# A new written order for a five-engine attention and feed-forward kernel, with five more summed sets

## The chip, the cores and the metric

The kernel runs on one core of a Trainium2 chip. Five engines work side by side from queues of their own: TensorE (PE in the profile; its weight loads PEld), VectorE (DVE), ScalarE (ACT), GpSimd (POOL), and SyncE (SP), which here issues nearly all DMAs. The metric is the device time of one execution in microseconds (us). Before the change three runs took 684.30, 684.40 and 684.44 us; the median is 684.4.

## The reference

Two branches work on the same x of 2048 rows and 640 columns and are mixed row by row:

```
g = sigmoid((x * gate_w).sum(-1))
a = softmax_attention(x @ wqkv, 32 heads of 20 columns) @ wo
h = x @ w1 + b1                       # 1536 columns
b = (h * tanh(softplus(h))) @ w2      # Mish
out = g * a + (1 - g) * b
```

The scores are 32 matrices of 2048 x 2048. Everything is bf16 on the way in and out.

## The kernel before

**Tiling.** Four heads make a quartet; there are 8 quartets and 4 query chunks of 512 columns, so 32 groups G of one quartet and one chunk. Within a group there are 16 key blocks j of 128 rows, and for each the four heads t. A *score tile* is one (G, j, t): a matmul with 32 weight rows and 128 weight columns that writes 128 x 512 values into one of seven PSUM banks (`score`, L1073). The heads of a quartet sit in four row groups of 32 of TensorE's array.

**Two ways to an exponential.** Most key blocks go to ScalarE: one activation (L1091, step `x`) reads one, two or three neighbouring banks and writes E in SBUF. Five or so blocks of every group, "sets", go to VectorE instead: `d_unit` (step `D`) makes the score tile and a tensor_scalar (L586) writes a scaled score as int16, whose bits read as bf16 are a power of two with a piecewise linear fraction. To come closer to the exponential, the kernel uses shifted copies of the int16 tile, made on GpSimd by adding a constant to four values at a time (L616, `add_shift`). A plain set uses the tile and two shifted copies as three right-hand sides, the copies with values of V scaled by fixed ratios (`VD`). A *summed* set adds the tile and its first copy on VectorE (L640, `total` in `d_sum`) and shifts the original once more, so it has two right-hand sides. The flag is the last number of a `d` step. A summed set has other constants (`SHIFT2`, `BETA2`).

**Products with V.** Step `V` (`emit_pv`, L1108) is four matmuls with 21 weight columns each, one per head, in four column groups of the array; they add into bank 7. The 21st column of V is one, so the row sum of the softmax comes with it. When the last product of a group is in, `normalise` puts four VectorE instructions and a store on record: a transpose (L1137), a reciprocal (L1144), a product (L1151) and the stores to `o_dram`.

**The rest of the matmuls** are in 184 chains: projections to q, k, v (`dense_chain`, `v_chain`, `first_k_chain`), w1 (`h_chain`), w2 (`b_chain`) and wo (`wo_chain`). Each chain fills one bank with 1 to 20 products (`product`, L663: four matmuls of 32 weight columns) and is then emptied by VectorE (L850 with the bias for w1, L752 for q and k, L808 for v, L895 for w2, L972 for wo). Mish runs twice on ScalarE over 12288 columns (L871, step `m`).

**The order** is written out by hand. A string, ORDER, is read step by step, and every step issues its instructions to the engines' queues in that order:

- `S2,4`: two score tiles for ScalarE into banks 4 and 5; `x2`: one activation over the two oldest of these
- `D24,14,3,6`: the score tile of group 24, block 14, head 3 into bank 6 for VectorE; `d24,13,0`: take a set
- `C5,6`: begin chain 5 in bank 6; `F`: its next product
- `V14,1`: the products of block 14 with right-hand side 1 (-1 is E)
- `y142`: the 142nd VectorE instruction that was put on record; `p31,6`: the 31st shift on GpSimd, into buffer 6 (-1 is in place)
- `l`, `q`, `k`, `o`, `b`, `e`: loads on SP's queue, `m`: Mish, `H`: products with zero weights

Each queue runs strictly in its order; an instruction waits until what it reads is written and what it overwrites has been read. So the string fixes what stands behind what on each of the engines.

The steps that matter below: `b1f`, the bias as f32, was made by a cast (L849) inside the emptying of the first w1 chain, directly ahead of L850. Its source `b1bf` is loaded by step `l2` (`load_late`, L487) together with the first tile of w1. In the string, group 23's reciprocal is `y767`, its L1151 `y771`; group 24's L1151 is `y803`.

Of the kernel before, what the change touches and what calls it, by code (L numbers as in the profile page):

```python
# [9 lines left out]
P = 128  # L10
ACT = mybir.ActivationFunctionType
ALU = mybir.AluOpType
F32 = mybir.dt.float32
# [6 lines left out]
S2,4 S2,2 C0,6 S2,0 x2 x2 F F F F F C1,5 F y1 y3 C2,4 F x2 y4 C3,5 S2,2 F x2 y5 C4,4 S2,0 F x2 y2 y6 C6,5 S2,2  # L20
x2 F F F F F F F d2,3,0 F F F F F F F F F F F F F C5,6 F F S2,0 S2,3 F F F x2 y7 d0,6,0 y8 y9 x2 y10 y11 y12
C7,2 F F F F F S2,0 x2 S2,5 C8,3 V0,-1 F F F F F F F F F F F F F F F F F F F F y13 y14 y15 x2 V1,-1 S3,0 C9,4
F F F F F S2,5 x3 x2 y16 d0,8,0 y17 y18 y19 d1,5,0 V2,-1 C10,6 V4,-1 S3,0 S2,3 V3,-1 V5,-1 F F F F F x3 x2 y20
C11,5 F S3,0 F F F F F d1,0,0 F F F F F F F D0,15,3,3 x3 D0,15,0,4 F F F F F F F C12,6 F F S3,0 F F F y21 y23
y24 y25 y26 y27 y22 x3 D0,15,2,5 S2,3 x2 y29 d3,4,0 y28 V6,-1 V7,-1 S3,0 C13,5 F F D0,14,3,6 S2,3 F F F x2 q1
y30 y31 x1 x2 C14,0 F F F V9,-1 D0,15,1,6 S2,1 F F F F F F F F F F F S2,3 D0,14,0,5 F V8,-1 y32 x2 q2 y33 x2
D0,14,1,6 S2,1 F F F F F y34 x2 y35 V10,-1 C15,6 S3,3 y36 y37 y38 y39 F F F F F D0,14,2,2 S2,0 F F F F F v0,0
V11,-1 V15,0 y44 y43 y40 p1,1 x3 x2 D1,15,1,5 S3,2 y41 y42 x3 V14,0 V15,1 y45 D1,15,0,6 y46 S2,0 V12,-1 C16,5
F F F F F F S3,2 D1,15,2,6 F F F F p2,7 p3,1 p4,6 d1,2,0 l0 y47 V14,1 V15,2 x2 x3 S2,0 D1,14,0,6 y48 y49 y50
C17,5 V14,2 V13,-1 D1,15,3,2 S2,3 d2,6,0 x2 y51 l1 F F F d1,1,0 x2 y52 D1,14,1,6 S2,0 F F x2 p5,7 S2,2  # L30
D1,14,2,4 x2 p6,8 y53 y54 y55 y56 l2 V0,-1 V1,-1 S2,0 D1,13,0,6 C18,5 F F S3,2 x2 y58 y57 F F F S2,0 D1,13,1,6
# [277 lines left out]
def kernel(  # L309
# [1087 lines left out]
```

## Time and profile before

| what | value |
| --- | --- |
| median of 3 runs | 684.4 us (684.30 to 684.44) |
| profiled execution, first to last instruction (span) | 681.8 us |
| median beyond the span | 2.6 us |
| PE busy | 672.8 us (99%) |
| ACT busy | 666.7 us (98%) |
| DVE busy | 597.3 us (88%) |
| POOL busy | 354.0 us (52%) |
| granted TensorE clock | 0.999 |

The page gives the span of the profiled execution and no other time of it; the 2.6 us are what the timed runs take beyond that span. In the timeline a row has the start, the length, the engine, the line, the operation, what it writes and reads, how often it stands in the row, and in brackets the idle time before it with what ended it. Neighbouring instructions of one line are merged into one row. Matmuls are pipelined: the next one starts well before the first has ended, so the distance of starts says more than lengths.

### The profile page before, as it was taken

How to read it: one execution, taken by the hardware profiler on the slowest of the kernel's cores; microseconds unless marked ns; L12 is line 12 of the kernel's file. 1: busy time of each engine (PE TensorE's matmuls, PEld its weight loads, DVE VectorE, ACT ScalarE, POOL GpSimd, SP SyncE). 2: the span in 40 equal slices, each digit the busy share in tenths (PEclk: the TensorE clock that was granted, in tenths of full speed). 3: DMA queues.
4: the chain of work that ended last, by engine and by line, in shares of the span. 5: the costliest groups of instructions: out<-in, count | busy, mean ns of one | idle time of the engine just before them, and what ended most of it. 6: DMA issues, size and time to landing. Idle time of an engine off the chain costs nothing.

```text
span 681.8 us, 24517 instructions
## 1 busy us (share of the span) xinstructions
PE 672.8 (99%) x10355; PEld 234.2 (34%) x10355; DVE 597.3 (88%) x1033; ACT 666.7 (98%) x692; POOL 354.0 (52%) x349
## 2 busy tenths in 40 slices
PE   8999999999999999999999999999999999999997
PEld 4433333323323443333333222222243333333334
DVE  5689989898999889899888988999999988799896
ACT  6999999999999999999999999999999999999996
POOL 5135446454454535565645654456646654466453
PEclk9999999999999999999999999999999999999999
DMA  8444322213312211111231223221232122131221
GB/s 171 118 89 126 81 43 53 53 38 63 89 26 52 49 44 36 26 35 34 43 97 33 43 53 74 64 55 33 56 92 60 21 48 29 41 66 35 60 87 60
DMA packets 128542, 40.47 MB, mean 59 GB/s; under 512 B 94960, under 2 KB 127872, under 8 KB 128432
## 3 DMA queue, kind: packets, MB, share of 16 engines
q1 hardware_dynamic: 126032, 38.29, 25.5%
q8 instruction: 81, 1.33, 0.9%
q10 hardware_dynamic: 2400, 0.62, 0.4%
q14 instruction: 29, 0.24, 0.1%
HBM read 22.29 MB, written 12.78 MB: 51 GB/s over the span
## 4 chain that ended last, share of the span: by engine, by line
PE 89%; ACT 7%; DVE 2%; issue 1%; POOL 0%; DVEq 0%; ACTq 0%
PE Sp L1108 30%; PE Sp L1073 30%; PE Sp L663 29%; ACT E L1091 5%; ACT big L871 2%; DVE T L586 0%; PE Sp L515 0%; PE Sp L1336 0%; DVE T L1151 0%; DVE ot L1353 0%; PE Sp L1217 0%; PE Sp L1123 0%; ACT L1091 0%; PE Sp L1199 0%; ACT big L966 0%
## 5 line engine op out<-in xcount | busy, mean ns | idle before, releaser
L1091 ACT ACTIVATE E<-Sp 128x1024 bf16<-128x1024 f32 (+2 forms) x674 | 634.7, 1127 | 4.4 <-PE Sp L1073 3.7
L616 POOL INT64_ADD T<-T x334 | 344.1, 1042 | 314.2 <-DVE T L586 208.5
L586 DVE TENSOR_SCALAR T<-Sp 128x512 int16<-128x512 f32 x668 | 440.2, 682 | 56.1 <-PE Sp L1073 45.7
L1073 PE MATMUL Sp<-qT,kT 32*128 32x512 bf16 x2048 | 259.5, 384 | 2.9 <-ACT E L1091 1.0
L1073 PEld LDWEIGHTS <-kT 32*128 32x128 bf16 x2048 | 70.1, 91 | 244.9 <-issue 240.4
L1108 PE MATMUL Sp<-E,VA 128*21 128x512 bf16 x1380 | 128.0, 382 | 0.0
L1108 PE MATMUL Sp<-T,VD 128*21 128x512 bf16 x1288 | 117.9, 382 | 0.1
L663 PE MATMUL Sp<-w_sb,big 128*32 128x320 bf16 x1536 | 72.9, 302 | 0.2 <-DVE T L586 0.2
L663 PE MATMUL Sp<-xT,w1t 128*32 128x512 bf16 x960 | 72.2, 382 | 0.0
L1108 PEld LDWEIGHTS <-VA 128*21 128x21 bf16 x2048 | 43.9, 90 | 57.3 <-issue 48.4
L1108 PE MATMUL Sp<-T,VA 128*21 128x512 bf16 x668 | 63.5, 382 | 0.0
L663 PE MATMUL Sp<-xT,ws 128*32 128x512 bf16 x720 | 52.2, 382 | 0.0
L1108 PEld LDWEIGHTS <-VD 128*21 128x21 bf16 x1288 | 29.8, 90 | 38.6 <-issue 32.6
L663 PEld LDWEIGHTS <-big 128*32 128x32 bf16 x1536 | 32.9, 95 | 29.0 <-issue 21.8
L850 DVE TENSOR_SCALAR big<-Sp,b1f 128x512 bf16<-128x512 f32 x48 | 35.6, 741 | 1.8 <-PE Sp L663 1.2
L663 PE MATMUL Sp<-wv,xT 128*32 128x81 bf16 (+2 forms) x960 | 31.0, 257 | 0.0
L663 PEld LDWEIGHTS <-w1t 128*32 128x32 bf16 x960 | 19.8, 95 | 25.4 <-issue 17.4
L752 DVE CAST st<-Sp 128x512 bf16<-128x512 f32 x36 | 24.5, 681 | 2.6 <-PE Sp L663 2.4
L663 PE MATMUL Sp<-wo_sb,od 128*32 128x320 bf16 (+1 forms) x608 | 26.3, 301 | 0.1
L1137 DVE STREAM_TRANSPOSE T<-Sp 128x512 f32<-128x512 f32 x32 | 22.7, 709 | 2.6 <-PE Sp L1108 2.4
L663 PEld LDWEIGHTS <-xT 128*32 128x32 bf16 x960 | 18.8, 96 | 10.8 <-issue 7.7
L663 PEld LDWEIGHTS <-ws 128*32 128x32 bf16 x720 | 15.3, 95 | 19.4 <-issue 12.1
(76 smaller groups left out, 196.8 us busy)
## 6 DMA issues: line engine op xcount, KB each, us to landing
w1t<-in_B_w_dram SPq DMA_DIRECT2D x24, 320.0 KB
q_dram<-st SPq DMA_DIRECT2D x20, 128.0 KB
b_dram<-bt SPq DMA_DIRECT2D x16, 160.0 KB
bl<-b_dram SPq DMA_DIRECT2D x16, 160.0 KB
qT<-q_dram SPq DMA_DIRECT2D x124, 20.0 KB
o_dram<-T SPq DMA_DIRECT2D x120, 20.0 KB
out_dram<-ot SPq DMA_DIRECT2D x15, 160.0 KB
kT<-k_dram SPq DMA_DIRECT2D x28, 80.0 KB
```

The lines of the kernel that those rows point to most:

```text
L586: nc.vector.tensor_scalar(out=dst.bitcast(I16), in0=src, scalar1=inv_sqrt_dh * LOG2E * 128.0, scalar2=127.0 * 128.0 + (BETA2 if two else B ...
L616: nc.gpsimd.int64_add(dst[:, :].bitcast(I64), src[:, :].bitcast(I64), n * 0x0001000100010001)
L663: nc.tensor.matmul(out_[k : k + 32], lhsT=lhsT[:, k : k + 32], rhs=rhs, tile_position=(0, k), **kw)
L752: nc.vector.tensor_copy(out=res["st"][:, :], in_=ps[:, :])
L850: nc.vector.tensor_scalar(out=big[:, pair_of(c, ft), (ft % 2) * QC : (ft % 2 + 1) * QC], in0=ps[:, :], scalar1=b1f[:, ft : ft + 1], scalar ...
L871: nc.scalar.activation(v, v, ACT.Mish)
L1073: nc.tensor.matmul(ps_cols, lhsT=kT[p][32 * t_ : 32 * t_ + 32, j * P : (j + 1) * P], rhs=qT[G][32 * t_ : 32 * t_ + 32, :], tile_position=( ...
L1091: nc.scalar.activation(E[:, x : x + n, :], allb[:, k0 : k0 + n, :], ACT.Exp, scale=inv_sqrt_dh,)
L1108: nc.tensor.matmul(acc[32 * t_ : 32 * t_ + DH + 1, :], lhsT=lhsT, rhs=rhs, start=(pv_done[G] == 0), stop=(pv_done[G] == pv_total[G] - 1), ...
L1137: nc.vector.transpose(out=st["T1"][:, :, :].rearrange("p b r -> p (b r)"), in_=acc[:, :])
```

## The change

The ORDER string is replaced as a whole: 5819 steps become 6236. Both have the same 1380 score tiles for ScalarE and 668 for VectorE, the same 184 chains with 1220 products, the same loads. What differs:

- the places of nearly all steps; 740 of the ScalarE score tiles are now steps of their own (`S1,3`), none were before
- 688 activations instead of 674: 55 over one bank, 574 over two, 59 over three (before 31, 580, 63)
- 17 summed sets instead of 12: (10,11) and (21,12) become plain, (1,15), (12,12), (13,11), (15,10), (22,11), (26,12) and (26,13) are summed
- 44 shifts on GpSimd in place instead of 13
- the bias cast is a VectorE instruction of its own, put on record by step `l2`, which stands earlier
- a chain knows its bank, so products of several chains can alternate (`F134 F144`), where before a chain ended before the next began
- the code can also run a product row group by row group (`run_part`, step `f`); the new ORDER has no such step

```diff
-S2,4 S2,2 C0,6 S2,0 x2 x2 F F F F F C1,5 F y1 y3 C2,4 F x2 y4 C3,5 S2,2 F x2 y5 C4,4 S2,0 F x2 y2 y6 C6,5 S2,2
-x2 F F F F F F F d2,3,0 F F F F F F F F F F F F F C5,6 F F S2,0 S2,3 F F F x2 y7 d0,6,0 y8 y9 x2 y10 y11 y12
...
-D3,10,1,2 D4,14,0,1 S2,5 q6 p32,1 x2 V11,0 F F S2,3 V11,1 V8,-1 y140 y141 p33,7 x2 y142 D4,15,1,6 D4,13,0,5
-S2,1 V11,2 V10,0 p34,2 y143 x2 S2,3 D4,15,2,0 y144 x2 y145 V10,1 V9,-1 S2,1 D4,14,1,6 C32,5 F V10,2 y146 x2
...
-F F F F x2 b6 y765 x2 D24,14,2,5 D24,14,1,4 S2,2 p249,3 x2 y767 y770 d24,0,0 y771 y766 d25,6,0 y769 y768 V15,0
-V0,-1 S2,0 D24,14,3,6 D24,14,0,4 y773 x2 S2,2 C135,5 F F F F S2,0 D24,13,2,4 x2 x2 d24,3,0 y772 y774 F F F F
...
-D25,13,1,5 S2,2 F V10,-1 S2,0 D25,13,2,4 F F F F y797 x2 y798 x2 y799 S2,2 D25,12,0,5 F F F S2,0 D25,13,3,4
-p259,0 p260,2 p261,5 p262,1 x2 y800 y801 y802 x2 F V15,0 V15,2 S2,2 D25,12,1,5 V1,-1 d25,8,0 V14,0 y804 x2
-S2,0 D25,12,2,6 D25,12,3,4 y803 y805 p263,2 x2 d25,6,0 V14,2 V15,1 D25,11,0,5 S2,2 y806 y807 x2 V2,-1 V0,-1
...
+S1,0 S1,2 x1 S1,3 S1,6 C0,1 x2 C1,0 S1,5 C2,2 C6,4 F0 F0 F0 F0 F0 y1 F F y2 x1 F1 F2 x1 S1,3 C4,5 S1,1 x1 S1,6
+F x1 F6 y3 C3,3 y4 y5 F y6 C8,3 x1 S3,0 x3 S1,5 F6 F6 C5,6 F6 F6 F F F6 F d0,8,0 x1 F6 F8 F6 F6 F6 F F8 F8 F6
...
+S3,0 D3,10,3,5 x2 x1 y134 V3,-1 V13,2 V4,-1 D3,12,2,6 C34,0 S2,3 V13,1 y20 F F y135 D4,15,0,5 x2 S1,1 x2 y122
...
+S1,5 D4,14,0,2 S1,6 F F y144 F S1,3 p31,6 p32,5 x2 S1,4 V11,0 p33,7 y145 y146 V8,-1 D4,13,0,5 x2 S2,1
+D4,15,1,6 x2 V11,1 V11,2 y148 y147 S1,3 D4,15,2,0 S1,4 p34,2 V10,0 V10,1 D4,14,1,6 y149 C32,5 x2 d4,6,1 S1,1
...
+y768 y767 p249,6 S1,5 x2 S2,2 S2,0 C132,6 F V10,2 F F F F F x2 F F F F F x2 y770 F S1,2 D24,14,1,4 S1,3 y769
+V0,-1 H D24,14,2,5 S1,0 y772 y773 S1,1 V15,0 d24,7,0 D24,14,0,4 x2 D24,14,3,6 y774 x2 S2,2 C135,5 F y775 F x2
+y776 F y771 F F D24,13,2,4 S2,0 F F d25,6,0 F S1,2 D24,13,0,6 S1,3 F y777 F p251,3 x2 p252,4 y778 F p250,-1
...
+D25,13,1,5 F y800 F p261,5 y801 F F D25,13,2,4 x2 S1,0 x2 S1,1 V10,-1 V11,2 F y802 y803 y804 S2,2 D25,12,0,5
+p262,1 F x2 F S1,0 d25,8,0 q28 D25,13,3,4 x2 S1,1 F y806 y807 F V15,0 F S1,2 D25,12,1,5 S1,3 V14,2 x2 V1,-1
+p260,-1 S1,0 y808 x2 D25,12,3,6 S1,1 D25,12,2,4 V15,2 V14,1 S2,2 y809 x2 p263,2 x2 D25,11,0,5 y810 d26,5,0
...
 class Chain:
 
 
-    def __init__(self, start, due, pieces, evac):
+    def __init__(self, start, due, n, fn, evac, last=None, cols=512):
         self.start, self.due = start, due
-        self.pieces = deque(pieces)
-        self.evac = evac
+        self.fn, self.evac, self.last = fn, evac, last
+        self.n, self.first, self.rows, self.told = n, True, {}, None
+        self.whole, self.top = 0, n
+        self.ps, self.cols = None, cols
+
+    def done(self):
+        return self.whole == self.top and all(len(r) == 4 for r in self.rows.values())
...
             if i == 2:
                 nc.sync.dma_start(b1bf, B_b1.rearrange("(ft p) -> p ft", p=P))
+                dve(lambda: nc.vector.tensor_copy(b1f, b1bf))
             load_w1(i - 2)
         else:
             ft = slice(2 * (i - 4), 2 * (i - 4) + 2)
...
+    def product(ch, out_, lhsT, rhs, row, start=None):
+        if start is None:
+            start, ch.first = ch.first, False
+        if row is not None:
+            r = slice(32 * row, 32 * row + 32)
+            mm = nc.tensor.matmul(
+                out_, lhsT=lhsT[r, :], rhs=rhs[r], tile_position=(32 * row, 0),
+                start=start, stop=ch.done(), skip_group_check=True,
+            )
+            if ch.told is not None:
+                tc.add_manual_dep(mm.ins, ch.told.ins.name, told, reason="parts of one bank")
+            if not ch.done():
+                ch.told = nc.sync.nop()
+                tc.add_manual_dep(ch.told.ins, mm.ins.name, told, reason="parts of one bank")
+            return
         for k in range(0, P, 32):
             nc.tensor.matmul(
-                out_[k : k + 32], lhsT=lhsT[:, k : k + 32], rhs=rhs, tile_position=(0, k), **kw
+                out_[k : k + 32], lhsT=lhsT[:, k : k + 32], rhs=rhs, tile_position=(0, k),
+                start=start, stop=ch.done(), skip_group_check=True,
             )
...
             def copy():
-                if (ft, c) == (0, 0):
-                    nc.vector.tensor_copy(b1f, b1bf)
                 nc.vector.tensor_scalar(
                     out=big[:, pair_of(c, ft), (ft % 2) * QC : (ft % 2 + 1) * QC], in0=ps[:, :],
                     scalar1=b1f[:, ft : ft + 1], scalar2=None, op0=ALU.add,
...
-    def run_piece():
-        ch = chain[0]
-        ch.pieces.popleft()()
-        if not ch.pieces:
-            ops, done = ch.evac()
+    def run(ch, k, row):
+        if ch.ps is None:
+            ch.ps = bank_ap(ch.bank, [P, ch.cols])
+        ch.fn(ch, k, row)
+        if ch.done():
+            if ch.last:
+                ch.last()
+            ops, done = ch.evac(ch)
             for f in ops[:-1]:
                 dve(f)
             dve(ops[-1], done)
+
+    def run_piece(i=None):
+        ch = chain[0] if i is None else chains[i]
+        ch.whole += 1
+        run(ch, ch.whole - 1, None)
+
+    def run_part(i, row):
+        ch = chains[i]
+        for k in sorted(ch.rows, reverse=True):
+            if row not in ch.rows[k]:
+                break
+        else:
+            ch.top -= 1
+            k = ch.top
+            ch.rows[k] = set()
+        ch.rows[k].add(row)
+        run(ch, k, row)
...
     def begin(k, bank):
-        chain[0], chain_bank[0] = chains[k], bank
+        chain[0] = chains[k]
+        chains[k].bank = bank
 
     steps = {
         "q": load_q,
         "V": emit_pv,
         "C": begin,
         "F": run_piece,
+        "f": run_part,
         "H": heat,
         "y": vector,
         "Y": vector,
```

More of the change, by code (lines that the diff above doesn't have):

```diff
@@ L668, in transpose_chain, with piece @@
         c, u = divmod(s, NU)
-        def piece():
-            ps = box["ps"] = bank_tile([P, KT * P], BF16)
+        def piece(ch, k, row):
+            ps = ch.ps = bank_ap(ch.bank, [P, KT * P], BF16)
             for kt in range(KT):
@@ L686, in evac @@
             return [copy], None
-        return Chain(start, due, [piece], evac)
+        return Chain(start, due, 1, piece, evac)
     strip_left = {}
@@ L760, in evac @@
             return [copy], done
-        return Chain(start, due, mm_pieces(KT, piece), evac)
+        return Chain(start, due, KT, piece, evac, last)
     def rows_in(kind, p):
@@ L861, in evac @@
             return [copy], done
-        return Chain(start, due, mm_pieces(KT, piece), evac)
+        return Chain(start, due, KT, piece, evac, last)
     act_q = deque()
```

669 lines of the change are left out of this document (335 added, 334 removed).

## The prediction

> **What bounds the kernel now.** I read the page first: busy shares, then the chain that ended last.
>
> ```profile
> span 681.8 us, 24517 instructions
> PE 672.8 (99%) x10355; PEld 234.2 (34%) x10355; DVE 597.3 (88%) x1033; ACT 666.7 (98%) x692; POOL 354.0 (52%) x349
> PE 89%; ACT 7%; DVE 2%; issue 1%; POOL 0%; DVEq 0%; ACTq 0%
> PE Sp L1108 30%; PE Sp L1073 30%; PE Sp L663 29%; ACT E L1091 5%; ACT big L871 2%; DVE T L586 0%; PE Sp L515 0%; PE Sp L1336 0%; DVE T L1151 0%; DVE ot L1353 0%; PE Sp L1217 0%; PE Sp L1123 0%; ACT L1091 0%; PE Sp L1199 0%; ACT big L966 0%
> ```
>
> Three matmul lines share 89% of the chain equally: TensorE's own queue sets the end, with ScalarE nearly as full and VectorE at 88%. A busy PE of 99% hides small waits, because the ends of matmuls are modelled. So I priced the queue by turns, from starts in the timeline. Four column-tiled matmuls (L1108, L663) run side by side as one product turn; up to four row-tiled score matmuls (L1073) as one score turn.
>
> ```profile
> 20.74 0.60 PE L1073 MATMUL Sp<-qT,kT 32*128 32x512 bf16 x5
> 21.27 0.61 PE L1108 MATMUL Sp<-E,VA 128*21 128x512 bf16 x8
> ...
> 300.26 0.61 PE L1108 MATMUL Sp<-T,VD 128*21 128x512 bf16 x8
> 300.70 0.39 PE L663 MATMUL Sp<-xT,ws 128*32 128x512 bf16 x4
> 301.02 0.39 PE L1073 MATMUL Sp<-qT,kT 32*128 32x512 bf16 x3
> 301.34 0.62 PE L663 MATMUL Sp<-xT,ws 128*32 128x512 bf16 x8
> ```
>
> Eight L1108 matmuls, two turns, take 300.70 - 300.26 = 0.44, so 0.22 a turn. The single turn at 300.70 takes 0.32, because a score turn follows: a change of kind costs 0.10. A score turn followed by a product turn also takes 0.32 (301.02 to 301.34). Five score matmuls, which need two turns, take 21.27 - 20.74 = 0.53: a second score turn in a row costs 0.21.
>
> Counted along the written order before: 649 score turns, 1280 product turns of 512 columns, 616 of 320, 160 narrower ones, four transposes, and 1277 changes of kind. A turn of 320 columns costs (232.89 - 232.21) / 5 = 0.136:
>
> ```profile
> 8.47 0.60 PE L1073 MATMUL Sp<-qT,kT 32*128 32x512 bf16 x6 [0.44 <-DVE qT L1236]
> ...
> 231.34 1.05 PE L663 MATMUL Sp<-xT,ws 128*32 128x512 bf16 x16
> 232.21 0.85 PE L663 MATMUL Sp<-wv,xT 128*32 128x320 bf16 x20
> 232.89 1.25 PE L663 MATMUL Sp<-xT,ws 128*32 128x512 bf16 x20
> ...
> 674.62 1.53 PE L1336 MATMUL Sp<-wo,O 128*128 128x320 bf16 x8
> ```
>
> 1929 x 0.22 + 616 x 0.136 + 1277 x 0.10 = 636; the 160 narrow turns, bounded by 0.136 each, add at most 22. So 636 to 658 of the 666 us between the first score turn (8.47) and the closing products (674.62) is TensorE's own work, and **8 to 30 us is waiting**. That is all an order can win; the start and the tail, 8.5 + 7.2 us, keep their code.
>
> **The change, part by part.** Times are against the profiled span of 681.8; the timed runs have a median of 684.4, 2.6 longer, which I carry over unchanged.
>
> Turns. Five more sets are summed: each loses one product turn on L1108 (three right-hand sides become two), 5 x 0.22 = 1.10 gained. Counted along the new order there are 652 score turns, three more at 0.21, 0.63 lost, and again exactly 1277 changes of kind, though 740 of the 1380 tiles for ScalarE are now issued singly (before none): most stay neighbours on TensorE's queue. Sum **-0.47**.
>
> The bias cast (L849) leaves the path. Before, it stood directly ahead of the first L850:
>
> ```profile
> 96.99 0.81 DVE L849 CAST b1f<-b1bf 128x12 f32<-128x12 bf16 x1
> 97.91 0.75 DVE L850 TENSOR_SCALAR big<-Sp,b1f 128x512 bf16<-128x512 f32 x1
> ...
> 98.18 0.90 PE L1073 MATMUL Sp<-qT,kT 32*128 32x512 bf16 x3
> 99.01 0.40 PE L1108 MATMUL Sp<-T,VD 128*21 128x512 bf16 x4
> ```
>
> L850 empties bank 0, and the third score of the turn at 98.18 writes bank 0: the turn lasts 0.90 instead of 0.39, 0.51 of waiting. In the new order the cast stands some 6 us of work earlier, between the emptying of a q/k product and the int16 cast (L586) of a score tile in bank 5. That bank is written again six turns and two changes, some 2.1, after it was filled; 0.75 (an emptying like L850's) + 0.81 + 0.62 (L586, from 2.47 for four, below) is 2.2, so some of it comes back: 0 to 0.4, all 0.81 if nothing covers it. I take 0.2. Its DMA and the first w1 tile's move well ahead on SP's queue, before the loads of q, k and further strips; the q tile they delay is not read until the second group. **-0.51 + 0.20**.
>
> Normalising behind the score casts. Twice VectorE does part of a normalisation ahead of score casts, and TensorE waits:
>
> ```profile
> 516.68 0.25 DVE L1144 RECIPROCAL rec<-T 128x16 f32<-128x16 f32 x1
> 516.85 1.16 DVE L640 TENSOR_TENSOR T<-T 128x2048 bf16<-128x2048 bf16 x1
> 517.93 0.48 DVE L1151 TENSOR_TENSOR T<-T,rec 128x320 bf16<-128x320 f32 x1
> 518.32 0.55 DVE L895 TENSOR_SCALAR bt<-Sp,g_t 128x320 bf16<-128x320 f32 x1
> 518.78 2.47 DVE L586 TENSOR_SCALAR T<-Sp 128x512 int16<-128x512 f32 x4
> 518.61 0.68 PE L1073 MATMUL Sp<-qT,kT 32*128 32x512 bf16 x3
> 519.52 0.39 PE L1073 MATMUL Sp<-qT,kT 32*128 32x512 bf16 x3 [0.23 <-DVE T L586]
> 520.11 0.73 PE L663 MATMUL Sp<-w_sb,big 128*32 128x320 bf16 x16 [0.20 <-DVE T L586]
> ...
> 540.32 2.28 POOL L616 INT64_ADD T<-T  x2 [1.33 <-DVE T L586]
> 540.50 1.21 DVE L1151 TENSOR_TENSOR T<-T,rec 128x320 bf16<-128x320 f32 x1
> 541.16 0.61 PE L1108 MATMUL Sp<-T,VD 128*21 128x512 bf16 x8
> 542.36 0.39 PE L1073 MATMUL Sp<-qT,kT 32*128 32x512 bf16 x3 [0.58 <-DVE T L586]
> ```
>
> From 518.61 to 520.11 two score turns and a change (0.53) take 1.50: 0.97 of waiting. The new order puts the reciprocal and L1151 behind the four casts, 0.25 + 0.48 = 0.73 sooner. At 541.16 two product turns and a change are 0.54; the score starts after 1.20: 0.66 waited. There L1151 moves some ten VectorE instructions later, well behind these casts. What is late next is the store of that output to o_dram, read by products a whole group later. **-0.73 - 0.66**.
>
> [...]
>
> The sums. A summed set trades a POOL shift for another, and adds one L640 on VectorE:
>
> ```profile
> L640 DVE TENSOR_TENSOR T<-T 128x2048 bf16<-128x2048 bf16 x12 | 14.5, 1210 | 0.6 <-POOL T L616 0.6
> ...
> 516.85 1.04 DVE T L640
> ```
>
> Five more make +6.05 on VectorE, 597 to 603 of 682. In the chain of waits, one of the twelve sums stands on the path, for 1.04 (the second line). Bounds: 0 when all five fall into VectorE's slack, 5 x 1.04 = 5.2 when none does. I take one in twelve: 5 x 1.04 / 12 = **+0.43**.
>
> Smaller activations. 688 instead of 674 for the same 1380 tiles: 580 pairs become 574, 63 triples 59, 31 singles 55.
>
> ```profile
> 151.38 7.17 ACT L1091 ACTIVATE E<-Sp 128x1024 bf16<-128x1024 f32 x9
> 663.61 9.32 ACT L1091 ACTIVATE E<-Sp 128x512 bf16<-128x512 f32 x10
> L1091 ACT ACTIVATE E<-Sp 128x512 bf16<-128x512 f32 x31 | 20.3, 668 | 0.1
> ...
> 14.79 1.94 ACT L1091 ACTIVATE E<-Sp 128x1024 bf16<-128x1024 f32 x2 [0.29 <-PE Sp L1073]
> 17.15 7.84 ACT L1091 ACTIVATE E<-Sp 128x1024 bf16<-128x1024 f32 x7 [0.42 <-PE Sp L1073]
> 25.54 15.13 ACT L1091 ACTIVATE E<-Sp 128x1536 bf16<-128x1536 f32 x15 [0.55 <-PE Sp L1073]
> ```
>
> By the written order the first run is three singles and six pairs, the second two singles, six pairs and two triples: nine activations over 15 tiles take 7.17, ten over 20 take 9.32, the last of each run some 0.2 longer than its turn: 0.09 an instruction and 0.41 a tile. So +14 cost 1.2 us of ScalarE; unoverlapped, by the single's mean, (668 - 410) ns x 14 = 3.6. Thirteen of the fourteen fall in the first group (41 activations for its 62 tiles instead of 28), where ScalarE now sits idle 0.29 + 0.42 + 0.55 = 1.26: cover and cost cancel. I take 0, bounds -1.3 and +3.6.
>
> The wait behind the first Mish stays: between the last score tile before the table load and the first one after it, the new order has 28 x 0.22 + 40 x 0.136 against 30 x 0.22 + 37 x 0.136, the same within 0.03.
>
> Sum: -0.47 - 0.51 + 0.20 - 0.73 - 0.66 + 0.43 = -1.74, so 680.1 for the span and **682.7** for the run.
>
> **The rivals.**
>
> *The waits move (0.26).* Buffers are unchanged, and both engines carry some 650 us of work; what is taken from one wait shows up at the next. Against it: each named wait has a particular instruction ahead of it that is gone. Then only the turns count: 684.4 - 0.47 = 683.9.
>
> *VectorE becomes the bound (0.20, slower).* The new sums stand between score casts in nearly every case, and each holds the PSUM banks behind it for 1.2 us. With three of the five on the path, 3.1, and no more won by the named waits: 684.4 - 0.5 + 3.1 = 687.0. It decides from the second sum that lands there (2.1 - 0.5 = +1.6). A harder form of it (0.05 of the 0.20): a sum starts while POOL is adding and is held, as L1151 at 540.50 was, by 1.21 - 0.48 = 0.73; then two sums on the path cost 2 x 1.77 = 3.5, so 687.4. [...] For the rival: the row on the chain. Against it: eleven of twelve sums cost nothing, and VectorE is at 88%.
>
> *Many small waits go too (0.13).* Nothing but rearrangement is needed to win more of the 8 to 30 us. If 2 of them go beside my sum: 680.7. For it: no view names most of these waits, and the new order reaches right across the kernel. Against it: the busy shares leave little room.
>
> *The change does nothing to the path:* covered by the first rival; the added piece-by-row code is not called by the new order.
>
> **How the numbers follow.** Forecast 0.41, its own range 681.8 to 683.6 (half of the gains kept or lost). About 0.2%, 1.4 us, is what can be told from no change: faster means under 683.0, slower over 685.8. The forecast falls in faster but for 0.08, the small-waits case wholly, and of the first rival 0.04: 0.33 + 0.13 + 0.04 = 0.50; same 0.08 + 0.22 = 0.30; slower 0.20. The range, to hold 8 in 10, goes from 679.8, a little beyond the small-waits case, to 685.9: of the VectorE rival, one or two sums on the path lie inside it.
>
> **What would show it.** Right: about 3316 matmuls on L1108; no score turn of 0.9 before the first L850's bank is reused; L640 x17 and still at most one or two in the chain; no wait on L586 near 518 and 541; ScalarE without its three idle stretches before 26 us. Wrong: L640 or L586 with several us of the chain (VectorE bound), or the same total of PE waiting under other lines (waits moved), or ScalarE's share of the chain grown in the first 40 us (singles cost more than 0.09).

## The result and the profile after

The new order is slower: 688.22 us median (687.77 to 689.40, 6 runs) against 684.42 for the kernel before on the same chip (6 runs), ratio 1.0055 with a 95% interval of 1.0043 to 1.0067. The profiled execution is the longest of the six: it spans 687.6 us, 5.8 more than the profile before, where the medians differ by 3.8; the spans of the other five are 686.0 to 687.3. Three single executions far outside the rest (779 us of the kernel before, 1966 of e5_open_after, 3177 of e7_sums_before) are left out of every median below.

The page after, first the span and the busy shares, then the chain that ended last by engine and by line:

```profile
span 687.6 us, 24488 instructions
PE 674.4 (98%) x10335; PEld 236.3 (34%) x10335; DVE 602.5 (88%) x1038; ACT 668.2 (97%) x706; POOL 355.6 (52%) x349
PE 59%; ACT 32%; issue 5%; DVE 3%; DMA 1%; ACTq 0%; DVEq 0%
ACT E L1134 30%; PE Sp L1151 19%; PE Sp L1116 19%; PE Sp L698 19%; DVE T L614 2%; ACT big L900 2%; DMA wv<-in_gate_w_dram 1%; PE Sp L1381 0%; PE Sp L543 0%; DVE T L1194 0%; DVE st L783 0%; ACT L1134 0%; DVE VD L596 0%; DVE T L668 0%; PE Sp L1242 0%
```

VectorE's 603 is where the prediction had it, and TensorE's busy time rose by only 1.6 of the 5.8 us: the rest is waiting. The chain now runs through ScalarE for 32%, before for 7%; the sums (L668) have 0% of it. The groups behind it (line, engine, operation; then busy us, mean ns; idle before, and what ended it):

```profile
L1134 ACT ACTIVATE E<-Sp 128x1024 bf16<-128x1024 f32 (+2 forms) x688 | 636.3, 1093 | 7.5 <-PE Sp L1116 6.6
L1116 PE MATMUL Sp<-qT,kT 32*128 32x512 bf16 x2048 | 258.6, 384 | 5.8 <-ACT E L1134 2.3
L1151 PE MATMUL Sp<-E,VA 128*21 128x512 bf16 x1380 | 129.7, 383 | 0.0
L1151 PE MATMUL Sp<-T,VD 128*21 128x512 bf16 x1268 | 117.4, 383 | 0.0
L1151 PE MATMUL Sp<-T,VA 128*21 128x512 bf16 x668 | 64.0, 382 | 0.0
L668 DVE TENSOR_TENSOR T<-T 128x2048 bf16<-128x2048 bf16 x17 | 20.6, 1209 | 0.2 <-POOL T L644 0.2
```

The counts are the forecast ones (1380 + 1268 + 668 = 3316 products with V, 17 sums). What grew is the idle time of the scores, 5.8 where it was 2.9. To find the places I laid each trace's matmuls along its written order and took the start of the last product with V of each group. After minus before, in us:

```
group            0     3     4    23    24    25    31
after         +2.56 +2.89 +5.13 +4.86 +7.25 +5.63 +5.66
```

Between these steps it is flat to some 0.5: the loss sits in three places.

**The opening (+2.56).** After, a v product waits for the gate column, and the next score tile stands behind it. TensorE's timeline after:

```profile
9.26 1.03 PE L698 MATMUL Sp<-xT,wkp 128*32 128x512 bf16 x16
11.66 0.26 PE L698 MATMUL Sp<-wv,xT 128*32 128x81 bf16 x8 [1.36 <-DMA wv<-in_gate_w_dram]
```

**Group 4 (+2.24).** The same view at 108 to 113 us, with VectorE and GpSimd:

```profile
108.56 2.28 POOL L644 INT64_ADD T<-T  x2 [0.92 <-PE Sp L1151]
108.61 1.33 DVE L1194 TENSOR_TENSOR T<-T,rec 128x320 bf16<-128x320 f32 x1
...
109.86 1.16 DVE L596 TENSOR_SCALAR VD<-VA 128x588 bf16<-128x588 bf16 x1
110.95 1.86 DVE L614 TENSOR_SCALAR T<-Sp 128x512 int16<-128x512 f32 x3
111.67 0.39 PE L1116 MATMUL Sp<-qT,kT 32*128 32x512 bf16 x3 [1.52 <-DVE T L614]
```

Group 3's normalising product takes 1.33 instead of 0.48, the scaling of V for pair 2 takes 1.16 where most take 0.32; the score casts behind them come late, and TensorE stands still for 1.52. Then the granted clock drops to 0.50 (windows of one us: PE, PEld, DVE, ACT, POOL busy, granted clock, DMA):

```profile
112.00:113.00 1.00, 1.00 (x14) 0.19 (x11) 0.81 (x2) 0.88 (x1) 0.09 (x1) 0.55 0.56 36
113.00:114.00 1.00, 1.00 (x11) 0.30 (x15) 0.44 (x1) 0.48 (x2) 1.00 (x2) 0.50 0.44 39
114.00:115.00 1.00, 1.00 (x15) 0.11 (x6) 0.70 (x2) 0.69 (x1) 0.96 (x1) 0.50 0.46 40
115.00:116.00 1.00, 1.00 (x14) 0.16 (x11) 0.76 (x2) 0.44 (x1) 0.00 (x0) 0.75 0.01 3
```

**Behind the second Mish (+2.4 at group 24, 1.6 of it given back).** The timeline at 508 to 529 us:

```profile
508.80 10.45 ACT L900 ACTIVATE big<-big 128x12288 bf16<-128x12288 bf16 x1
...
519.67 0.60 PE L1116 MATMUL Sp<-qT,kT 32*128 32x512 bf16 x5
520.13 1.28 ACT L1134 ACT_TABLE_LOAD   x1 [0.89 <-PE Sp L1116]
...
526.87 2.28 POOL L644 INT64_ADD T<-T  x2 [5.58 <-DVE rec L1187]
526.89 1.36 DVE L1194 TENSOR_TENSOR T<-T,rec 128x320 bf16<-128x320 f32 x1
...
528.17 1.27 DVE L614 TENSOR_SCALAR T<-Sp 128x512 int16<-128x512 f32 x2
528.19 0.39 PE L1116 MATMUL Sp<-qT,kT 32*128 32x512 bf16 x1
528.90 0.39 PE L1116 MATMUL Sp<-qT,kT 32*128 32x512 bf16 x2 [0.32 <-DVE T L614]
```

Mish ends at 519.25, but the score tile that the next activation needs is issued late, so the table load stands idle for 0.89. Then group 23's normalising product takes 1.36, and the scores wait again.

Of the waits that the prediction named, the one ahead of the first use of the bias (before at 98.18) and the one of 541 are gone. The one of 518 only moved: group 23's product now stands behind the four casts, at 526.89, and the scores wait behind it at 528.

### The profile page after: what moved, and what is told of

Its sections match the earlier page's. It is cut to its first block, busy times and chain, and to the rows that moved or that the text cites. A ratio compares the mean times of both kernels' runs of the same rounds, so it can differ in the third digit from the quotient of the medians.

```text
span 687.6 us, 24488 instructions
## 1 busy us (share of the span) xinstructions
PE 674.4 (98%) x10335; PEld 236.3 (34%) x10335; DVE 602.5 (88%) x1038; ACT 668.2 (97%) x706; POOL 355.6 (52%) x349
## 3 DMA queue, kind: packets, MB, share of 16 engines
q8 instruction: 81, 1.33, 0.9%
## 4 chain that ended last, share of the span: by engine, by line
PE 59%; ACT 32%; issue 5%; DVE 3%; DMA 1%; ACTq 0%; DVEq 0%
ACT E L1134 30%; PE Sp L1151 19%; PE Sp L1116 19%; PE Sp L698 19%; DVE T L614 2%; ACT big L900 2%; DMA wv<-in_gate_w_dram 1%; PE Sp L1381 0%; PE Sp L543 0%; DVE T L1194 0%; DVE st L783 0%; ACT L1134 0%; DVE VD L596 0%; DVE T L668 0%; PE Sp L1242 0%
## 5 line engine op out<-in xcount | busy, mean ns | idle before, releaser
L1151 PE MATMUL Sp<-E,VA 128*21 128x512 bf16 x1380 | 129.7, 383 | 0.0
L698 PE MATMUL Sp<-w_sb,big 128*32 128x320 bf16 x1536 | 79.4, 302 | 0.0
L698 PE MATMUL Sp<-xT,w1t 128*32 128x512 bf16 x960 | 75.5, 385 | 0.0
L698 PE MATMUL Sp<-xT,ws 128*32 128x512 bf16 x720 | 54.9, 382 | 0.0
L698 PEld LDWEIGHTS <-big 128*32 128x32 bf16 x1536 | 34.5, 95 | 29.9 <-issue 21.8
L698 PE MATMUL Sp<-wv,xT 128*32 128x81 bf16 (+2 forms) x960 | 37.1, 257 | 1.7 <-DMA wv<-in_gate_w_dram 1.4
L698 PE MATMUL Sp<-wo_sb,od 128*32 128x320 bf16 (+1 forms) x608 | 28.5, 300 | 0.2
L698 PEld LDWEIGHTS <-xT 128*32 128x32 bf16 x960 | 21.6, 96 | 15.5 <-issue 8.1
```

The costliest lines, as they stand in the source:

```text
L698: nc.tensor.matmul(out_[k : k + 32], lhsT=lhsT[:, k : k + 32], rhs=rhs, tile_position=(0, k), start=start, stop=ch.done(), skip_group_chec ...
L1151: nc.tensor.matmul(acc[32 * t_ : 32 * t_ + DH + 1, :], lhsT=lhsT, rhs=rhs, start=(pv_done[G] == 0), stop=(pv_done[G] == pv_total[G] - 1), ...
```

## The experiments

Ratios are against the kernel before on the same chip, where its median was 683.95 to 684.26. In the orders of after, `y155` and `y777` are the normalising products of groups 3 and 23, `y771` is group 23's reciprocal, and `y142` and `y143` are the two scalings of V for pair 2.

### The late places

**e2_c3_after.** Group 3's normalising product and the first scaling of V behind later score casts:

```diff
-V3,-1 y155 S1,1 y142 y162
+V3,-1 S1,1 y162
...
-y166 d5,5,0 y167 x2
+y166 y155 d5,5,0 y167 y142 x2
```

> The kernel after the change, with two VectorE instructions moved behind the score casts that follow them: group 3's normalising product (it took 1.33 at 108.6 us beside GpSimd's adds, against 0.48 elsewhere) and one scaling of V (1.16 at 109.9, against a mean of 0.34). Theory of the places: the PE wait of 1.6 at 109.76 goes, and with it the stretch of half clock from 112 to 115.4 us, some 1.2 us more; 685.4 to 687 for the run (less where a timed run had no slow clock). Theory of the sums: nothing was summed there, so no more than 0.5 faster. If the two instructions are held by GpSimd's adds wherever they stand, they take over 1 us in the new place too, without a PE wait.

686.67 us (686.35 to 687.18), ratio 1.0036 (1.0023 to 1.0049), 1.55 less than after. Group 4 ends at +2.89 instead of +5.13 and the clock stays at 1.00. Part of that is the clock alone: in c_after_again, which has after's order and no fall of the clock there, the step at group 4 is 0.77, and here it is 0.11. So the place itself is worth 0.66, and the fall of the clock 1.5 more in the runs that have it. The product has not escaped GpSimd: at its new place it takes 1.05.

**e3_mish_after.** The second score tile of group 24 directly behind the first, ahead of other work:

```diff
-S1,4 D24,15,3,2 D24,15,2,6
+S1,4 S1,5 D24,15,3,2 D24,15,2,6
...
-p249,6 S1,5 x2
+p249,6 x2
```

> The kernel after the change, with one score tile, (24,0,1), issued directly behind (24,0,0), before two score tiles for VectorE and five products. The activation behind the second Mish needs both tiles, and the table load stands idle 0.9 us behind Mish until the second one is there. Theory of the places: the table load starts directly behind Mish, the wait of 1.26 at 521.9 shrinks by 0.9, 687.3 for the run. Theory of the sums: group 24's sum (1.18 at 521.4) is what holds the path there, so the wait stays and the run is within 0.3 of 688.2.

687.16 us (686.55 to 688.66), ratio 1.0050 (1.0037 to 1.0064): 1.06 less by the medians, only 0.3 by the ratios, and the intervals overlap, so the timed runs don't decide it. The profile does: the step at group 24 falls from 2.39 to 1.17, though group 23 ends 0.36 later. Beside c_after_again, which starts from the same +2.29 at group 0 and has its clock at 1.00 too, e3 ends at +3.12 instead of +3.90, 0.78 sooner.

### The opening

**e1_gate_after.** The gate column's DMA on ScalarE's queue right behind the first v weights:

```diff
+nc.scalar.dma_start(out=wv0[:, :, 0 : 4 * DH], in_=wrows[:, :, 2 * D : 2 * D + 4 * DH])
+nc.scalar.dma_start(out=wv0[:, :, 4 * DH : 4 * DH + 1], in_=gate_w.rearrange("(kt p o) -> p kt o", p=P, o=1))
```

> The kernel after the change, with one DMA issued earlier: the gate column (one column of the first v weights, 640 packets of 2 bytes) goes out on ScalarE's queue right behind the first v weights instead of behind the copy of q, some 4.5 us sooner. Theory of the places (the loss of 3.8 us comes from a few single waits: 1.5 at 9.91 us for this column, a collision of VectorE and GpSimd at 109 us with a slow TensorE clock behind it, and an idle ScalarE behind the second Mish): the wait of 1.4 on the gate column is gone and the run is 1.4 to 2.5 faster than the changed kernel, 685.7 to 686.8. Theory of the sums (VectorE is late all over because of five more sums): no effect on the sum of the other waits; the 1.4 us come back elsewhere in the first 40 us, within 0.5 of 688.2. Theory of the single-tile activations (ScalarE bounds the first group): the same, within 0.5 of 688.2.

688.31 us (687.58 to 689.43), ratio 1.0061 (1.0049 to 1.0074). The wait is gone, but the first score starts at 9.06 instead of 8.51, because the first product for q now waits 1.08 for a copy on ScalarE's queue, and the opening ends only 0.28 sooner. That only traded one delay for another, so the wait was taken away a second way.

**e10_gate2_after.** The first three products of that v chain behind the twelfth score tile:

```diff
-F0 F0 F0 F0 F0 y1 F F y2 x1 F1 F2 x1 S1,3
+F0 F0 F0 F0 F0 y1 y2 x1 F1 F2 x1 S1,3
...
-F x1 F6 y3
+F x1 y3
...
-x1 S3,0 x3 S1,5 F6 F6 C5,6
+x1 S3,0 x3 S1,5 F6 F6 F6 F6 F6 C5,6
```

> The kernel after with the first three products of the first v chain issued behind the twelfth score tile instead of ahead of the sixth, so that no score tile stands behind the wait for the gate column. If that wait (1.36 us in the profile, 0.5 to 0.9 in three other runs) holds up the opening: group 0's last product with V 0.5 to 1.3 earlier than 40.75 to 41.0, and 687.0 to 687.7. If ScalarE's single activations and their order hold it anyway: 688.2.

687.97 us (687.56 to 688.19), ratio 1.0052 (1.0040 to 1.0065). In its profile the wait of 1.36 is gone, but TensorE waits 0.27 and 0.74 elsewhere, at 16 and 27 us, with no releaser shown. By the timed runs the gate column isn't what the opening loses by; my theory of it fell.

**e8_split_before.** Before, its first 13 pairs split:

```diff
-S2,4 S2,2 C0,6 S2,0 x2 x2
+S2,4 S2,2 C0,6 S2,0 x1 x1 x1 x1
```

> The kernel before with its first 13 two-bank activations each split into two of one bank, in place: the opening then has 41 activations to the 62nd tile as the kernel after has, in the order of before. If ScalarE's number of instructions sets the opening: two singles start 2 x 0.476 apart where a pair took 0.903, so 13 x 0.05 = 0.6 us, with 0.09 an instruction 1.2 us: group 0's last product with V at 39.1 to 39.7 instead of 38.46, total 685.0 to 685.6. If cover and cost cancel (the prediction's step): 38.5 and 684.4. If the order and not the number makes the 2.56 us: under 0.3 us.

684.11 us (683.81 to 684.85), ratio 0.9999 (0.9989 to 1.0008). In its profile tile 37 is reached 18.78 us after the first activation, in the two profiles of before after 17.99 and 18.27, so the 12 splits up to there cost 0.5 to 0.8, 0.04 to 0.07 each. That is less than the prediction's 0.09: back to back, activations of one and two banks start 0.476 and 0.903 apart, so a split costs 2 x 0.476 - 0.903 = 0.05. In the timed runs nothing is left of it. The next run shows how little one profile says of the opening.

**c_before_again.** No edit.

> The kernel before once more, unchanged, for its opening: three runs whose first 30 us have the order of before had group 0's last product with V at 39.7 us, the profile of before at 38.46. If the opening of before differs from run to run with the landing of its transfers: between 38.4 and 39.8, and the 2.56 us of the opening are then in part the luck of one profile. If the order of the three runs made it: 38.46 again.

684.39 us (one run). Group 0's last product stands at 39.25 us, 0.79 later than in the first profile, and every group after it by 0.78 to 0.80. So the opening of before varies: 38.46, 39.25, and in six other runs with its order (in e8 with the pairs split) 39.66 to 41.02. The latest, e9's 41.02, has a clock of 0.50 from 28.0 to 31.4 us; without it they end at 39.96. The profile of before that the sum was made against had the luckiest opening; its span of 681.8 compares with a median of 682.5 over 26 timed runs.

**e5_open_after and e5b_open_after.** The first 66 score tiles in the order of before, after's order behind them (two runs of one kernel; the traces below are of the second):

```diff
-S1,0 S1,2 x1 S1,3 S1,6 C0,1 x2 C1,0 S1,5 C2,2 C6,4
+S2,4 S2,2 C0,6 S2,0 x2 x2 F F F F F C1,5 F y1 y3 C2,4
```

> The kernel after, but its first 66 score tiles (up to group 0's last product with V, about 44 us) issued in the order of the kernel before; everything behind that as in the kernel after. Theory of places (the opening's 2.56 us are ScalarE's and the order's, and nothing later makes them up): group 0's last product with V at 38.5 instead of 41.0 us, and 688.2 - 2.6 = 685.6 us, ratio about 1.002. Rival one (only the wait for the gate column counts, and the run that took that wait away gained 0.27): 687.9. Rival two (the groups behind have slack of their own and the opening was hidden): 688.2.

> The kernel after with the opening order of the kernel before up to score tile 66, a second time, for its profile: 686.0 us. If the opening's loss lies in tiles 37 to 62: ScalarE from tile 37 to tile 63 in 11.8 us with 12 activations without a gap, and group 0's last product with V 0.8 earlier than in the kernel after whatever the transfer does. If it lies ahead of tile 37: that stretch equal, and tile 37 1 to 2 us earlier.

685.89 us (ten runs, 685.23 to 686.46), ratio 1.0022 (1.0013 to 1.0031), and 686.40 (five runs, 685.75 to 688.30), ratio 1.0041 (1.0027 to 1.0055).

**c_after_again.** No edit, on the chip of e5b.

> The kernel after once more, unchanged: 688.0 to 688.2 us; group 0's last product with V between 40.7 and 41.3 us as in the five profiles with this opening; ScalarE from the start of the activation of tile 37 to that of tile 63 12.65 us with 15 activations, as in the profile after.

687.81 us (687.37 to 688.24), ratio 1.0055 (1.0042 to 1.0069). So the opening is worth 1.4 us beside e5b, where the granted clock fell in two of the five runs, and 2.3 by e5's ratio. ScalarE's timeline in c_after_again (x is the number of activations):

```profile
8.71 2.49 ACT L1134 ACTIVATE E<-Sp 128x512 bf16<-128x512 f32 x4 [1.17 <-PE Sp L1116]
12.61 15.39 ACT L1134 ACTIVATE E<-Sp 128x512 bf16<-128x512 f32 x22 [1.41 <-PE Sp L1116]
28.16 14.59 ACT L1134 ACTIVATE E<-Sp 128x512 bf16<-128x512 f32 x17 [0.16 <-PE Sp L1116]
```

The same view of e5b:

```profile
8.93 5.60 ACT L1131 ACTIVATE E<-Sp 128x1024 bf16<-128x1024 f32 x6 [1.18 <-PE Sp L1113]
...
17.18 7.84 ACT L1131 ACTIVATE E<-Sp 128x1024 bf16<-128x1024 f32 x7 [0.41 <-PE Sp L1113]
25.57 1.45 ACT L1131 ACTIVATE E<-Sp 128x1536 bf16<-128x1536 f32 x1 [0.55 <-PE Sp L1113]
28.38 13.79 ACT L1131 ACTIVATE E<-Sp 128x1024 bf16<-128x1024 f32 x14 [1.37 <-PE Sp L1113]
```

Both reach tile 37 at the same time, 28.16 and 28.38: whatever the first half loses to the gate column or to singles is covered, in the order of before by a wait of its own. TensorE's timeline of e5b:

```profile
25.39 0.61 PE L695 MATMUL Sp<-xT,ws 128*32 128x512 bf16 x8
27.50 0.40 PE L695 MATMUL Sp<-xT,ws 128*32 128x512 bf16 x4 [1.49 <-issue]
```

It lies between the fourth and the fifth product of one q chain, whose new operand there is the fifth part of xT. The view names no releaser, and it isn't that part's DMA: its record has it landed by 21.2 us. What stands ahead of the wait is a transfer of 16 KB on queue q8, which the DMA view calls "instruction", from 25.00 to 26.15. Sixteen profiles (all but that of e5_open_after) have eleven waits of TensorE over 0.1 us without a releaser between 12 and 670 us, 0.15 to 1.49 long and all before 40 us. Each of them ends 1.29 to 1.57 us after the end of such a transfer, and a span has only 81 of these, in after about one for 255 of its 20670 matmuls and weight loads. So TensorE may be waiting there for its own instructions; no run moved these transfers, so that is a coincidence in time and not a shown cause. In the eight profiles with that opening the wait was 0 to 1.49 us.

Behind tile 37 the last rows have the same 30 tiles in both: 14.59 us with 17 activations against 13.79 with 14. By the distances of starts (0.476, 0.903 and 1.330 for one, two and three banks) 3 more are 0.15; the other 0.65 are five activations that start 0.10 to 0.22 late, because ScalarE and the scores wait for each other in turn (in after's trace two score turns wait 0.49 and 0.13 for an activation, at 34.11 and 37.34). From the activation of tile 37 to that of tile 63 it is 12.64 to 12.66 us in all eight profiles of after's opening, and 11.83 or 11.84 in five with the order of before. The other three have a reason of their own: in e8 (12.09) one activation more, in e6 (13.01) scores that wait for a q tile, in e9 (13.16) the halved clock. So **0.8 us of the opening are the order in tiles 37 to 62**. The rest, 0.6 to 1.5 by the medians, is not shown; from profile to profile the first half varies with the waits for q8 and with the start of the first activation (8.71 to 9.49).

### The places together

**e6_three_after.** e2, e3 and e5 in one.

> The kernel after with three places undone together: the opening of the kernel before, group 3's normalising product and the first scaling of V of pair 2 behind the next two score casts, and the score tile (24,0,1) directly behind (24,0,0) ahead of the second Mish. If the three places are all that the change lost and they add: 688.2 - 2.6 - 1.55 - 1.05 = 683.0 us, ratio 0.998: the rest of the change then did what the prediction said of it (its forecast was 682.7). If the waits only move when one is taken away: 685 or more. If the clock's slow stretch near 113 us and not the order made the difference in the single repairs: about 684.5.

684.54 us (683.87 to 685.32), ratio 1.0007 (0.9998 to 1.0016): between the theories, 1.5 above the sum. Two of the waits had only moved. Its timeline of VectorE and GpSimd:

```profile
110.11 2.05 POOL L641 INT64_ADD T<-T  x2 [0.56 <-DVE T L611]
...
111.45 1.05 DVE L1191 TENSOR_TENSOR T<-T,rec 128x320 bf16<-128x320 f32 x1
...
522.26 3.30 POOL L641 INT64_ADD T<-T  x3 [4.29 <-DVE rec L1184]
522.28 1.36 DVE L1191 TENSOR_TENSOR T<-T,rec 128x320 bf16<-128x320 f32 x1
```

Where e2 had put it, group 3's product meets the next addition (1.05), and group 23's still takes 1.36. By the distances of starts TensorE loses 0.58 + 0.29 and 0.72 behind them.

**e11_best.** e6, with group 3's product behind both scalings of V and group 23's reciprocal and product ahead of the last score cast of their set, the one that lets GpSimd start (so not behind all four casts, as in the change):

```diff
-y166 y155 d5,5,0 y167 y142 x2 ... y143 y169
+y166 d5,5,0 y167 y142 x2 ... y143 y155 y169
...
-y774 x2 S2,2 C135,5 F y775 F x2 y776 F y771
+y774 y771 x2 S2,2 C135,5 F y775 y777 F x2 y776 F
```

> The kernel after with the three places undone, and two normalising products moved off GpSimd's additions: group 3's behind both scalings of V of pair 2 (it still took 1.05 beside an addition where the run with three places had put it), group 23's (1.36 beside an addition) ahead of the last cast of set (24,14), so that it runs before GpSimd's next addition can start. In the run with three places TensorE waited 0.58 and 0.29 at 112.6 to 113.5 and 0.72 at 523.6. If these waits are the normalising products': 684.5 - 1.5 = 683.0, ratio 0.998. If they move: 684.5.

**683.06 us (682.51 to 684.22), ratio 0.9984 (0.9975 to 0.9992)**: 1.1 less than before by the ratio, and 5 less than after, as expected. Its timeline at the three spots:

```profile
112.22 0.33 DVE L593 TENSOR_SCALAR VD<-VA 128x588 bf16<-128x588 bf16 x1
...
113.30 0.48 DVE L1191 TENSOR_TENSOR T<-T,rec 128x320 bf16<-128x320 f32 x1
...
515.04 1.28 ACT L1131 ACT_TABLE_LOAD   x1
...
521.11 0.48 DVE L1191 TENSOR_TENSOR T<-T,rec 128x320 bf16<-128x320 f32 x1
```

Each is back at its plain length, and the table load has no idle time ahead of it.

**e12_late_after.** e11, but with after's own opening.

> The kernel after with its own opening, but all repairs behind it: group 3's normalising product behind both scalings of V of pair 2, the score tile ahead of the second Mish, group 23's reciprocal and normalising product ahead of the last cast of set (24,14). If the places add up: 683.06 + 2.1 = 685.2 us, and 688.1 - 2.9. If the opening is hidden once the late waits are gone: 683.5.

684.75 us (684.17 to 685.45), ratio 1.0011 (1.0003 to 1.0020): 3.06 less than c_after_again on the same chip, and by the ratios 1.9 more than e11. The late places and the opening add.

### Single parts of the change

**e9_bias_before.** Before, with the bias cast as an instruction of its own, earlier:

```diff
-F F F y133 y134 x2
+F F F y134 y58 y135 x2
```

(The numbers behind an inserted instruction shift by one; `y58` is the cast.)

> The kernel before with one part of the change alone: the bias cast issued early, behind a score cast some 5 us ahead of its use, as in the kernel after. The prediction's step: the wait of 0.51 us at 98.2 leaves TensorE's path, 0.2 comes back elsewhere, so 684.2 - 0.3 = 683.9. If the wait only moves to the next bank (a wait of 0.35 stands at 95.3 in the profile after): 684.2 and group 4's end at the place of before against the groups ahead of it.

683.73 us (683.10 to 685.66), ratio 0.9991 (0.9982 to 1.0000). Its profile stands at +2.56 against before at group 2 and at +1.97 at group 4, and so to the end: 0.59 won in between. The median's 0.5 lies at the edge of its interval. VectorE's timeline shows the cast at a fifth of its former length:

```profile
92.96 0.16 DVE L493 CAST b1f<-b1bf 128x12 f32<-128x12 bf16 x1
```

So the step was right, and worth more than the 0.31 given it: the wait did not move. The former 0.81 was itself a collision, for an addition had begun 0.25 us ahead of the cast at 96.99:

```profile
94.71 4.08 POOL L616 INT64_ADD T<-T  x4 [1.28 <-DVE T L586]
```

**e4_plain_after.** Seven newly summed sets plain again; for one of them:

```diff
-y422 p124,-1 F D12,11,2,6 ... V12,0 ... V12,1
+V12,0 p124,-1 F D12,11,2,6 ... V12,1 V12,2
```

> The kernel after the change, with the seven newly summed sets made plain again: seven VectorE sums (8.5 us of VectorE) go, seven product turns come back (7 x 0.22 = 1.5 us of TensorE), GpSimd has as many adds as before; the first product of five of these sets is issued some steps earlier, since the last copy is made in place. It computes with the plain sets' constants. Theory of the places: the sums cost little, so the run is 0.5 to 2 slower than the changed kernel, 688.7 to 690.2. Theory of the sums (three of five on the path for 1.04 each): 1.5 - 3.1 = 1.6 faster, 686.6.

693.59 us (692.25 to 694.08), ratio 1.0134 (1.0120 to 1.0147), 5.4 more. Its page names 1.7 us of waits for a shift of GpSimd, where after has none; the seven turns more are 1.5, and its profile ends 4.1 later than after's:

```profile
L1151 PE MATMUL Sp<-T,VD 128*21 128x512 bf16 x1296 | 119.8, 384 | 1.7 <-POOL T L644 1.7
```

**e7_sums_before.** Before, with the same seven sets summed; for that one:

```diff
-V12,0 V6,-1 S3,0 x2 y420 ... p124,0 ... V12,2 ... V12,1
+y421 V6,-1 S3,0 x2 p124,-1 y422 ... V12,0 ... V12,1
```

> The kernel before with one part of the change alone: the same seven sets summed that the change sums newly (1,15), (12,12), (13,11), (15,10), (22,11), (26,13), (26,12), each with one more VectorE addition and one product turn fewer; nothing else moved, and the two sets that the change takes back stay summed. If sums earn what the run with plain sets lost: between 7 x 0.22 = 1.5 us (the turns alone) and 5 us less than 684.4, so 679.4 to 682.9. If the added 7 x 1.04 us on VectorE count (the prediction's term): one in twelve on the path, 684.4 - 1.5 + 0.6 = 683.5. If VectorE is the bound: 684.4 + 3 or more. The places are set by hand, so a product may wait for its sum once or twice (about 0.5 us each).

689.47 us (four runs, 688.25 to 689.97), ratio 1.0074 (1.0060 to 1.0088), 5.2 more than before. Its timeline at two of the seven:

```profile
288.00 1.22 DVE L640 TENSOR_TENSOR T<-T 128x2048 bf16<-128x2048 bf16 x1
...
289.87 0.39 PE L1073 MATMUL Sp<-qT,kT 32*128 32x512 bf16 x3 [0.90 <-DVE T L586]
...
309.91 1.23 DVE L640 TENSOR_TENSOR T<-T 128x2048 bf16<-128x2048 bf16 x1 [1.17 <-POOL T L616]
...
311.79 0.39 PE L1073 MATMUL Sp<-qT,kT 32*128 32x512 bf16 x3 [1.26 <-DVE T L586]
```

Taking the sums out and putting them in cost nearly the same, likely because either edit leaves an order that was fitted to the other: once a product waits for a shift, once a score waits behind a sum with its whole length. What a sum earns in a place made for it stays open; that it costs 0.9 to 1.3 us where it stands ahead of a score cast is shown.

## Why the prediction was wrong

The forecast was 682.7, the result 688.22; the range ended at 685.9. By the medians: without the late places after is 3.06 faster (e12), without its opening another 1.9 (e11 against e12, by the ratios), and what is then left of the change is 1.1 faster than before. The sum had -1.74 for just that part. **Two steps failed above all. Normalising: group 23's moved product was priced at its plain 0.48 and group 3's not at all, without asking what GpSimd does at the new places; beside its additions they took 1.36 and 1.33, and the late places, the second Mish among them, cost 3.06. Smaller activations, put at 0: the new opening costs 1.4 to 2.3, of which 0.8 are shown to lie in tiles 37 to 62.**

- **Turns, -0.47.** The matmuls came out as counted. Right.
- **Bias, -0.51 + 0.20.** Right in mechanism, 0.3 too cautious (e9: 0.59 in the profile, 0.5 in the median). The 0.20 rested on the cast keeping its 0.81; at the new place it takes 0.16. (The 2.1 for six turns and two changes is also 6 x 0.22 + 2 x 0.10 = 1.5 by the prediction's own prices.)
- **Normalising behind the score casts, -0.73 - 0.66.** Most of what stood to be won there can be won, though not at the place that the change gives it: in e11, with group 23's product ahead of the last cast, the difference to before falls from +1.07 at group 23 to -0.14 at group 25, 1.2 of the 1.39. At the place that the change gave it, this is the step that failed. I said that what is late next is the store, and left it at that: a moved instruction was priced by its plain 0.48 and I did not ask what GpSimd does at its new place. Group 23's landed 0.02 after an addition had begun, and took 1.36. I had a row for it (1.21 at 540.50, 0.18 after an addition had begun), and used it only to price the sums.
- **Nothing was asked of the normalising products that the prediction did not name.** Group 3's stood at a new place too, in the same kind of collision, with a scaling of V behind it that was held as well. That place alone is worth 1.3 to 1.55 in the timed runs (e2): 0.66 in the profiles, and 1.5 more where the clock falls.
- **The Mish wait stays.** I compared the work between the tiles at the first Mish. At the second the next tile had gone behind more work: 0.89 idle, 0.78 between the profiles (e3).
- **Smaller activations, 0.** The price of an instruction was too high, 0.09 for 0.05 (12 splits cost 0.5 to 0.8 in e8), and the failure lies in the cover. Cover was counted in the first 26 us only; the second half, tiles 37 to 62, has none, and there the new order costs 0.8, mostly by late starts that no count of instructions shows.
- **Sums, +0.43.** In the change itself they have 0% of the chain. My size for them was small enough not to matter.
- **The baseline.** Each timed run takes some 1.8 us beyond its own span. The other 0.8 of the 2.6 was the luck of the opening in the one profile of before, whose span lay that much under the usual one; it is no constant that can be carried over.

Of the rivals, the harder form of "VectorE becomes the bound" came nearest in time (687.4), which is luck, for its two held sums did not happen (0% of the chain); its mechanism, a VectorE instruction held by an addition of GpSimd, did happen, but to normalising products (1.33 and 1.36 for 0.48). "The waits move" (683.9) had the right doubt and no place. The sign for "singles cost more", ScalarE's share of the chain, was a poor one: in the first 40 us it grew from 9% to 18%, but in c_before_again, the kernel before, it is 19%.

## What to carry to other kernels

Here, where GpSimd is busy for 52% of the span, a moved normalising product had two prices, its plain 0.48, and up to 1.36 where an addition of GpSimd was already under way, and a scaling of V 0.32 or, beside one, 1.16; look up what GpSimd does at the new place, and what stands behind the instruction on its queue, since three such products were held in the kernel before too, and one of them cost a wait over 0.4. Price a new order by its places, with the same instant laid side by side in both traces, and not by counts: here all counts were right, and three spots made the result. And take a second profile of the kernel before, for what differs between two of them (0.8 us here) is no term of a sum.

## What the runs showed of the hardware

**In these traces the first to start held the other.** Of 31 normalising products in after, 16 overlap an addition by a third of their length or more, and nine of these take 0.482 or less. Two rows at 149 us of after:

```profile
149.54 0.47 DVE L1194 TENSOR_TENSOR T<-T,rec 128x320 bf16<-128x320 f32 x1
149.72 2.30 POOL L644 INT64_ADD T<-T  x2 [1.72 <-DVE T L614]
```

Here VectorE began first and lost nothing; GpSimd's two additions take 2.30 instead of 2 x 1.04. At 526.87 GpSimd began 0.02 earlier, and VectorE paid 0.88. Over the sixteen profiles it comes out as a sum: a product that began 0.40, 0.35, 0.18, 0.05 or 0.02 us after an addition (1.04 long) took 0.98, 1.03, 1.21, 1.33 or 1.36 (in before at 262.06, 600.59 and 540.50, in after at 108.61 and 526.89), its plain 0.48 and the rest of the addition less 0.14. Products that began 0.10 or more ahead of one kept their 0.48. Between these lies a row of after at 479.44: it began 0.04 ahead of an addition, 0.98 behind the start of the one before, and took 0.49. How sharp the edge is stays open. The scaling of V, with one input, took 0.32 alone and 1.16 at 109.86, 0.17 after an addition had begun.

**Behind some waits of 1.2 to 1.5 us the clock was halved.** In after, e4 and e5b the granted clock fell to 0.50 for some 3.4 us behind the wait at 110 us (in after 1.52 without a matmul, with matmuls on both sides, and 0.50 from 112.09 to 115.50); in e1, e3, e10 and c_after_again, with the same wait, it stayed at 1.00. Group 4's step is 2.24 to 2.26 where it fell and 0.75 to 0.77 where it didn't, so the fall costs 1.5. It also fell in e1 behind a wait of 1.19 at 523 us (six other traces with that wait kept their clock) and in e9 behind one of 1.38 at 26 us. The changes of the clock in after's trace, at 112.09, 115.50 and, behind the last instruction, 688.94 us, lie 3.413 and 573.44 us apart, the second 168 times the first. What decides whether the clock falls stays open.
